# Loading and multiplying the last chunk of an output projection in two parts (8 and 4 rows per partition)

## The chip, the cores and the metric

The kernel runs on one core of one Trainium2 chip. The metric is the device time of one execution in microseconds (us), the median of several. Three runs of the kernel before gave 296.84 us (296.07 to 297.12).

The traced run of the kernel before, from which all lines of "before" come, is 297.04 us, with a span of 295.2 us. The three jobs of experiments ran on three different chips (2, 12 and 1 in the record), so kernels are compared within a job.

## The reference

It is one decode step: attention over the last 2048 positions of a cache for 32 heads of width 192 and a batch of 2, then a gated feed-forward layer.

```python
x = A_x                                                   # [2, 1, 640]
h = x + attention(layernorm(x), k_cache, v_cache, wq) @ wo      # wo: [6144, 640]
h2 = h + (gelu(n @ w_gate) * (n @ w_up)) @ w_down         # n = layernorm(h), F = 1536
```

## The kernel before

All weights and cache tiles stream through one SBUF ring on one DMA queue, in the order in which they are used. `wo` is cut into four chunks `J` of 8 heads, each loaded by one DMA: 128 partitions, 12 rows of 640 bf16 per partition (15360 B). The last two chunks come behind the last V tile, and the feed-forward weights follow them.

```python
load_wo(2)
load_wo(3)
load_ffn()           # gate, up (15360 B per partition each), down in 4 parts of 3840 B

def load_wo(J):
    load(("wo", J), 2 * 12 * D, A_wo[1536 * J:1536 * (J + 1), :].rearrange("(p kk) n -> p kk n", kk=12),
         lambda v: v.rearrange("p (kk n) -> p kk n", kk=12))
```

`oproj(J)` adds the chunk's 24 small matmuls into one PSUM tile. The first waits for the whole chunk.

```python
def oproj(J):
    wo, wtoks = where["wo", J]
    def fn(e):
        # ... (J == 0 adds the residual)
        for kk in range(12):
            for h in range(2):
                r = 2 * (kk % 2) + h
                ins = e.matmul(m1[32 * r:32 * r + 2, 192:512], lhsT=ot[:, J % 2, kk, :],
                               rhs=wo[:, kk, 320 * h:320 * (h + 1)], start=..., stop=...,
                               tile_position=(0, 32 * r), skip_group_check=True)
        return ins
    pe(fn, R=wtoks + [("ot", J % 2), "xrow", "identb"], X=["m1"])
    # ...
```

The tail of the program is a serial chain: `o_rows(3)`, `oproj(2)`, `o_columns(3)` (which writes `ot`), `oproj(3)`, the row of h (`hrow`), its transposes (`h_columns`), layernorm (`hnT`), gate matmuls, residual matmuls, up matmuls, down matmuls, the copy `yrow`, and the output.

Of the kernel before, what the change touches and what calls it, by code (L numbers as in the profile page):

```python
# [13 lines left out]
D = 640  # L14
# [136 lines left out]
def bass_sequential_preLN__sliding_block_cached__geglu_ffn__decode_kernel(  # L151
# [12 lines left out]
    with ExitStack() as ctx:  # L164

        def sb(name, shape, dt):
            return ctx.enter_context(nc.sbuf_tensor(name, shape, dt))

        def ps(name, shape, dt):
            return ctx.enter_context(nc.psum_tensor(name, shape, dt))  # L170
# [4 lines left out]
        identb = sb("identb", [128, 128], BF16)  # L175
# [27 lines left out]
        xrow = sb("xrow", [128, D], BF16)  # L203
# [24 lines left out]
        ot = sb("ot", [128, 2, 12, B], BF16)  # L228
# [11 lines left out]
        m1 = ps("m1", [128, 512], F32)  # L240
# [6 lines left out]
        where, live, queue, used = {}, [], [], set()  # L247

        def load(key, nbytes, src, shape):


            if pos[0] + nbytes > RING:
                pos[0] = 0
            off, i = pos[0], pos[1]
            pos[0], pos[1] = off + nbytes, i + 1
            queue.append((key, off, nbytes, src, shape, i))

        def pump():
            while queue:
                key, off, nbytes, src, shape, i = queue[0]  # L260
                old = [q for q in live if q[1] < off + nbytes and off < q[1] + q[2]]
                if any(q[0] not in used for q in old):
                    return
                for q in old:
                    live.remove(q)
                queue.pop(0)
                live.append((key, off, nbytes))
                v = shape(ring[:, off // 2:(off + nbytes) // 2])
                toks = [("ring", x) for x in range(off // GRAN, (off + nbytes + GRAN - 1) // GRAN)]
                where[key] = (v, toks)  # L270
                P.op("sp", lambda e, v=v, src=src: e.dma_start(v, src), W=toks + [("sem", i % NSEM)],  # L271
                     dma=f"d{i % NSEM}")

        def done(*keys):
            used.update(keys)
            pump()
# [14 lines left out]
                load(("wq", i), 2 * (c1 - c0) * HQ * DH, wq[:, c0:c1, :], lambda v: v.rearrange("p (c n) -> p c n", n=HQ * DH))  # L291

        def load_wo(J):
            load(("wo", J), 2 * 12 * D, A_wo[1536 * J:1536 * (J + 1), :].rearrange("(p kk) n -> p kk n", kk=12),
                 lambda v: v.rearrange("p (kk n) -> p kk n", kk=12))

        def load_ffn():
            for key, w in (("wg", B_w_gate), ("wu", B_w_up)):
# [8 lines left out]
        def dve(fn, R=(), W=(), X=()):  # L307
            return P.op("dve", fn, R, W, X)
# [4 lines left out]
        def pe(fn, R=(), W=(), X=()):  # L313
            return P.op("pe", fn, R, W, X)
# [10 lines left out]
        def tt(out, a, b, op):  # L325
            return lambda e: e.tensor_tensor(out=out, in0=a, in1=b, op=op)  # L326
# [5 lines left out]
        for g in range(NG):  # L332
            if g > 0 and g + 1 < NG:
                load_k(g + 1)
            load_v(g)
            if g % 4 == 3 and g < NG - 5:
                load_wo(g // 4)
        load_wo(2)
        load_wo(3)
        load_ffn()  # L340
        pump()
# [43 lines left out]
        def _x_T(e):  # L385
# [11 lines left out]
            R=["pi"] + [("bits", k) for k in range(11)], W=["pti"])  # L397
# [211 lines left out]
            dve(lambda e: e.tensor_copy(ot[:, J % 2, :, :].rearrange("p k b -> p (k b)"), m2[:, 0:24]), W=[("ot", J % 2)], X=["m2"])  # L609

        def oproj(J):
            wo, wtoks = where["wo", J]

            def fn(e):
                if J == 0:
                    for h in range(2):
                        e.matmul(m1[32 * h:32 * h + 2, 192:512], lhsT=identb[0:2, 0:2], rhs=xrow[0:2, 320 * h:320 * (h + 1)],
                                 start=True, stop=False, tile_position=(0, 32 * h), skip_group_check=True)
                for kk in range(12):
                    for h in range(2):  # L620
                        r = 2 * (kk % 2) + h
                        ins = e.matmul(m1[32 * r:32 * r + 2, 192:512], lhsT=ot[:, J % 2, kk, :],  # L622
                                       rhs=wo[:, kk, 320 * h:320 * (h + 1)], start=(kk == 1 or J > 0 and kk == 0) and J < 3,
                                       stop=(J != 2 and kk >= 10), tile_position=(0, 32 * r), skip_group_check=True)
                return ins

            pe(fn, R=wtoks + [("ot", J % 2), "xrow", "identb"], X=["m1"])
            done(("wo", J))
            if J == 0:
                dve(lambda e: e.tensor_copy(hrow[0:98, :], m1[0:98, 192:512]), W=["hrow"], X=["m1"])  # L630
            if J == 1:
                dve(tt(hrow[0:98, :], m1[0:98, 192:512], hrow[0:98, :], ALU.add), R=["hrow"], W=["hrow"], X=["m1"])
            if J == 3:
                dve(lambda e: e.tensor_tensor_reduce(out=hrow[0:98, :], in0=m1[0:98, 192:512], in1=hrow[0:98, :], scale=1.0, scalar=0.0,
                                                     op0=ALU.add, op1=ALU.add, accum_out=rs[0:98, :]), R=["hrow"], W=["hrow", "rs"], X=["m1"])
# [19 lines left out]
        for g in range(NG):  # L655
            nxt = g + 1 < NG
            J = g // 4 - 1 if g % 4 == 0 and g > 0 else None
            if nxt:
                transposes(g + 1, 0)
            e_columns(g)  # L660
            if g % 4 == 3:
                z_rows(g // 4)
            if J is not None:
                o_columns(J)
            if nxt:
                transposes(g + 1, 1)
            if J is not None and J < 2:
                oproj(J)
            pv(g)
            if nxt:  # L670
                scores(g + 1)
            if g % 4 == 3 and nxt:
                o_rows(g // 4)
            if nxt:
                softmax(g + 1)
        o_rows(3)
        oproj(2)
        o_columns(3)
        oproj(3)

        h_columns()
# [49 lines left out]
        for i, (f0, f1) in enumerate(WDC):  # L731
            wd, wtoks = where["wd", i]
# [11 lines left out]
        for b, q in ((0, "sp"), (1, "act")):  # L744
            P.op(q, lambda e, b=b: e.dma_start(out[b, 0, :].rearrange("(r n) -> r n", r=4), yrow[b:b + 97:32, :]),
                 R=["y"], W=[("out", b)], dma=f"dout{b}")
# [59 lines left out]
```

## Time and profile before

Three lines of the page of the kernel before: the granted TensorE clock in tenths of full speed and the DMA share in 40 slices, and then the shares of the chain of waits that ended last.

```profile
PEclk9995959997979689977998697979599979599555
DMA  7999999999999999999999999999999999999991
...
DMA 69%; PE 24%; DVE 4%; issue 1%; SPq 1%; ACT 0%; DVEq 0%; ACTq 0%
```

The DMA stream is full from the second slice to the 39th, and the chain that ended last is mostly waiting for it. A change that leaves the bytes alone can only gain where the stream is almost over. The clock is at half speed there, in the last three slices.

The timeline of the kernel before, a few lines of the last 20 us. The columns are start (us from the span's start), duration (us), engine, source line, operation, output and inputs with their shapes, count, and in brackets the idle time before it and what ended that.

```profile
274.81 0.18 DVE L609 CAST ot<-m 128x24 bf16<-128x24 f32 x1 [2.11 <-PE m L605]
...
277.07 1.77 PE L622 MATMUL m<-ring,ot 128*2 128x320 bf16 x24 [2.31 <-DMA ring<-in_A_wo_dram]
...
278.89 0.49 DVE L634 CUSTOM_DVE_ANT_0 hrow<-m,hrow 98x320 f32<-98x320 f32 x1 [3.90 <-PE m L622]
...
287.17 1.83 PE L691 MATMUL ops<-ring,hnT 128*2 128x384 bf16 x20
...
290.76 1.77 PE L737 MATMUL m<-ring,uT 128*2 128x160 bf16 x48 [0.35 <-DVE uT L326]
...
292.58 0.33 DVE L743 CAST yrow<-m 98x160 bf16<-98x160 f32 x1 [1.88 <-PE m L737]
```

`ot` is complete at 274.99. TensorE then has nothing to do until the last `wo` chunk is there, and its 24 matmuls fill 1.77 us ahead of `hrow`. The up matmuls (L691 into `ops`) and the down matmuls (L737) show no DMA as their releaser: their weights were there in time.

When each load is complete does not stand in a line of the profile. I read it from the trace as the last of the 16 semaphore increments of each DMA. The Trainium skill ("DMA: Bandwidth & Descriptors", Why a DMA increments its semaphore by 16 and not by 1) says that only the full 16 mean that all the data is there. For the last `wo` chunk here they come between 273.37 and 276.94 us, and the matmuls start at 277.07.

| landing, us | wo 2 | wo 3 | gate | up | down 1 | down 2 | down 3 | down 4 |
|---|---|---|---|---|---|---|---|---|
| before | 272.34 | 276.94 | 281.53 | 286.15 | 287.35 | 288.50 | 289.65 | 290.81 |

### The profile page before, as it was taken

The numbers are of one execution on the slowest core, as the hardware profiler recorded it, in microseconds if no ns is written. First come the engines' busy times: TensorE is split into PE (matmuls) and PEld (weight loads), VectorE is DVE, ScalarE is ACT, GpSimd is POOL, SyncE is SP. The second block draws the span as 40 slices with busy tenths as digits, with TensorE's granted clock in tenths as the row PEclk, the third lists the DMA queues.
The fourth block names the chain that finished last, engine by engine and source line by source line (L and its number), as shares of the span: only waits on it lengthen the run. The fifth ranks groups of instructions, "written<-read, shape, count | busy, mean of one in ns | idle before, by whom it ended". The sixth has DMA issues, their size and how long they took to land.

```text
span 295.2 us, 4895 instructions
## 1 busy us (share of the span) xinstructions
PE 194.2 (66%) x2141; PEld 152.0 (51%) x2141; DVE 130.2 (44%) x326; ACT 95.6 (32%) x119; POOL 2.7 (1%) x19
## 2 busy tenths in 40 slices
PE   2483467749486398749581686767697667685664
PEld 1461165719284385538450656564666464653332
DVE  5950555615256154435353352525266435254022
ACT  2150134614233063516251323434344334241000
POOL 3000000000000000000000000000000000000000
PEclk9995959997979689977998697979599979599555
DMA  7999999999999999999999999999999999999991
GB/s 277 433 441 437 431 426 422 426 422 433 435 419 442 426 440 426 426 420 426 428 430 426 435 436 425 430 435 426 426 425 436 432 430 425 430 420 424 426 388 73
DMA packets 6521, 122.61 MB, mean 415 GB/s; under 512 B 738, under 2 KB 740, under 8 KB 1252
## 3 DMA queue, kind: packets, MB, share of 16 engines
q1 hardware_dynamic: 6488, 122.29, 97.1%
q8 instruction: 17, 0.28, 0.4%
q14 instruction: 4, 0.03, 0.0%
q10 hardware_dynamic: 12, 0.00, 0.0%
HBM read 122.29 MB, written 0.00 MB: 414 GB/s over the span
## 4 chain that ended last, share of the span: by engine, by line
DMA 69%; PE 24%; DVE 4%; issue 1%; SPq 1%; ACT 0%; DVEq 0%; ACTq 0%
DMA ring<-in_A_k_cache_dram 50%; PE tps L474 17%; DMA ring<-in_A_wo_dram 10%; DMA ring<-in_A_wq_dram 9%; PE m L622 1%; PE ops L572 1%; DVE rq L326 1%; PE m L737 1%; PE sps L691 1%; PE m L605 1%; SPq L271 1%; PE ops L691 1%; PE tps L702 1%; DVE ktr L486 0%; PE m L641 0%
## 5 line engine op out<-in xcount | busy, mean ns | idle before, releaser
L474 PE MATMUL tps<-identf,ring 128*128 128x128 f32 x768 | 115.3, 319 | 50.0 <-DMA ring<-in_A_k_cache_dram 49.3
L474 PEld LDWEIGHTS tps<-identf,ring 128*128 128x128 f32 x768 | 107.2, 168 | 52.7 <-DMA ring<-in_A_k_cache_dram 50.6
L483 ACT ACTIVATE ktr<-tps 128x1024 bf16<-128x1024 bf16 x80 | 79.3, 1023 | 90.5 <-PE tps L474 90.0
L486 DVE COPY ktr<-tps 128x1024 bf16<-128x1024 bf16 x112 | 74.1, 688 | 77.5 <-PE tps L474 76.9
L547 ACT ACTIVATE eexp<-sm,nm 128x512 bf16<-128x512 f32 x16 | 11.5, 721 | 65.2 <-DVE nm L545 65.2
L572 PE MATMUL ops<-ring,ering 128*32 128x384 bf16 x512 | 23.7, 327 | 3.8 <-DMA ring<-in_A_v_cache_dram 3.7
L536 DVE CUSTOM_DVE_ANT_1 sm<-sps,mska 128x512 f32<-128x512 f32 x16 | 11.1, 691 | 34.2 <-PE sps L530 34.2
L530 PE MATMUL sps<-ktr,rq 128*16 128x512 bf16 x384 | 24.8, 390 | 0.3 <-DVE rq L326 0.3
L572 PEld LDWEIGHTS ops<-ring,ering 128*32 128x32 bf16 x512 | 12.4, 96 | 12.1 <-DMA ring<-in_A_v_cache_dram 5.7
L530 PEld LDWEIGHTS sps<-ktr,rq 128*16 128x16 bf16 x384 | 9.4, 88 | 10.7 <-issue 1.0
L543 PE MATMUL m<-mrhs,pm 128*128 128x16 bf16 x16 | 2.9, 183 | 18.1 <-DVE mrhs L322 18.1
L543 PEld LDWEIGHTS m<-mrhs,pm 128*128 128x128 bf16 x16 | 1.5, 96 | 25.8 <-DVE mrhs L322 25.8
L496 PE MATMUL tps<-ring,xnT 128*32 128x384 bf16 x80 | 5.1, 406 | 6.8 <-DMA ring<-in_A_wq_dram 6.8
L326 DVE TENSOR_TENSOR rq<-ops,mask 128x96 bf16<-128x96 f32 x16 | 2.7, 249 | 12.8 <-PE ops L514 12.8
L622 PE MATMUL m<-ring,ot 128*2 128x320 bf16 x96 | 5.3, 371 | 3.9 <-DMA ring<-in_A_wo_dram 3.9
L326 DVE TENSOR_TENSOR ering<-m,mask 128x256 bf16<-128x256 f32 x16 | 6.7, 419 | 2.5 <-PE m L556 2.4
L496 PEld LDWEIGHTS tps<-ring,xnT 128*32 128x32 bf16 x80 | 2.2, 114 | 9.5 <-DMA ring<-in_A_wq_dram 7.9
L378 ACT ACTIVATE lt<-m,eps_t 128x2 f32<-128x2 f32 x2 | 0.5, 262 | 20.2 <-PE m L376 20.2
L556 PE MATMUL m<-sel,eexp 128*128 128x64 bf16 x64 | 4.8, 202 | 1.2 <-ACT eexp L547 1.2
L556 PEld LDWEIGHTS m<-sel,eexp 128*128 128x128 bf16 x64 | 4.4, 106 | 1.6 <-DVE nm L545 1.3
L326 DVE TENSOR_TENSOR orow<-m,wm 128x1536 bf16<-128x1536 f32 x3 | 5.3, 1750 | 0.0
L622 PEld LDWEIGHTS m<-ring,ot 128*2 128x2 bf16 x96 | 2.3, 95 | 5.7 <-issue 2.5
(112 smaller groups left out, 80.7 us busy)
## 6 DMA issues: line engine op xcount, KB each, us to landing
ring<-in_A_k_cache_dram SPq DMA_DIRECT2D x16, 3072.0 KB, 27.5
ring<-in_A_v_cache_dram SPq DMA_DIRECT2D x16, 3072.0 KB, 29.8
ring<-in_A_wo_dram SPq DMA_DIRECT2D x4, 1920.0 KB, 30.9
ring<-in_A_wq_dram SPq DMA_DIRECT2D x2, 3072.0 KB, 21.0
ring<-in_B_w_gate_dram SPq DMA_DIRECT2D x1, 1920.0 KB, 33.9
ring<-in_B_w_up_dram SPq DMA_DIRECT2D x1, 1920.0 KB, 24.5
ring<-in_B_w_down_dram SPq DMA_DIRECT2D x4, 480.0 KB, 26.4
ring<-in_A_wq_dram SPq DMA_DIRECT2D x1, 1536.0 KB, 27.9
```

The costliest lines, as they stand in the source:

```text
L326: return lambda e: e.tensor_tensor(out=out, in0=a, in1=b, op=op)
L474: ins = e.transpose(tps[bi][:, 128 * u:128 * (u + 1)], kv[:, off:off + 128], identf[:, :])
L483: act(lambda e, dst=dst, bv=bv: e.activation(out=dst, in_=bv, func=ACT.Copy), W=[("kt", slot, n)], X=[("t", bi)])
L486: dve(lambda e, dst=dst, bv=bv: e.tensor_copy(dst, bv), W=[("kt", slot, n)], X=[("t", bi)])
L496: ins = e.matmul(tps[0][32 * r:32 * (r + 1), 0:384], lhsT=xnT[:, c, 32 * J:32 * (J + 1)], rhs=wq[:, c - c0, 1536 * J + 384 * r:1536 * J + ...
L530: ins = e.matmul(sps[32 * ch:32 * ch + 16, :], lhsT=rq[:, g, k, :], rhs=ktr[:, g % 2, k // 2, 1024 * ch + k % 2:1024 * (ch + 1):2], start= ...
L536: dve(lambda e: e.tensor_tensor_reduce(out=sm[:, :].rearrange("p (u x) -> p u x", u=4), in0=sps[:, :].rearrange("p (u x) -> p u x", u=4), ...
L547: act(lambda e: e.activation(out=eexp[:, :], in_=sm[:, :], func=ACT.Exp, bias=nm[:, 0:1], scale=1.0, accum_out=zr[:, g // 4 % 2, g % 4:g % ...
L556: ins = e.matmul(o, lhsT=eexp[:, 128 * u:128 * (u + 1)], rhs=sel64[:, :], start=True, stop=True)
L572: ins = e.matmul(ops_[32 * r:32 * (r + 1), 0:384], lhsT=ering[:, g % 4, t, :], rhs=vv[:, 384 * t:384 * (t + 1)], start=(g % 4 == 0 and t < 4),
L622: ins = e.matmul(m1[32 * r:32 * r + 2, 192:512], lhsT=ot[:, J % 2, kk, :], rhs=wo[:, kk, 320 * h:320 * (h + 1)], start=(kk == 1 or J > 0 a ...
L691: ins = e.matmul(bank[32 * r:32 * r + 2, 0:384], lhsT=hnT[:, c, :], rhs=wv[:, c, 384 * r:384 * (r + 1)], start=(c == 0), stop=(c == NC5 - ...
```

## The change

The intent is to multiply 8 of the 12 rows while the other 4 are still coming. The last chunk becomes two DMAs into adjacent parts of the ring, and `oproj` two groups of matmuls, each waiting for its own part.

```diff
         def load_wo(J):
-            load(("wo", J), 2 * 12 * D, A_wo[1536 * J:1536 * (J + 1), :].rearrange("(p kk) n -> p kk n", kk=12),
-                 lambda v: v.rearrange("p (kk n) -> p kk n", kk=12))
+            src = A_wo[1536 * J:1536 * (J + 1), :].rearrange("(p kk) n -> p kk n", kk=12)
+            for i, (k0, k1) in enumerate(wo_parts(J)):
+                load(("wo", J, i), 2 * (k1 - k0) * D, src[:, k0:k1, :], lambda v: v.rearrange("p (kk n) -> p kk n", n=D))
+
+        def wo_parts(J):
+            return ((0, 12),) if J < 3 else ((0, 8), (8, 12))
 ...
         def oproj(J):
-            wo, wtoks = where["wo", J]
+            for i, (k0, k1) in enumerate(wo_parts(J)):
+                wo, wtoks = where["wo", J, i]
 ...
-                for kk in range(12):
+                    for kk in range(k0, k1):
 ...
-                                       rhs=wo[:, kk, 320 * h:320 * (h + 1)], ...
+                                           rhs=wo[:, kk - k0, 320 * h:320 * (h + 1)], ...
 ...
-            pe(fn, R=wtoks + [("ot", J % 2), "xrow", "identb"], X=["m1"])
-            done(("wo", J))
+                pe(fn, R=wtoks + [("ot", J % 2), "xrow", "identb"], X=["m1"])
+                done(("wo", J, i))
```

More of the change, by code (lines that the diff above doesn't have):

```diff
@@ L611, in oproj, with fn @@
         def oproj(J):
-            wo, wtoks = where["wo", J]
-            def fn(e):
-                if J == 0:
-                    for h in range(2):
-                        e.matmul(m1[32 * h:32 * h + 2, 192:512], lhsT=identb[0:2, 0:2], rhs=xrow[0:2, 320 * h:320 * (h + 1)],
-                                 start=True, stop=False, tile_position=(0, 32 * h), skip_group_check=True)
-                for kk in range(12):
-                    for h in range(2):
-                        r = 2 * (kk % 2) + h
-                        ins = e.matmul(m1[32 * r:32 * r + 2, 192:512], lhsT=ot[:, J % 2, kk, :],
-                                       rhs=wo[:, kk, 320 * h:320 * (h + 1)], start=(kk == 1 or J > 0 and kk == 0) and J < 3,
-                                       stop=(J != 2 and kk >= 10), tile_position=(0, 32 * r), skip_group_check=True)
-                return ins
-            pe(fn, R=wtoks + [("ot", J % 2), "xrow", "identb"], X=["m1"])
-            done(("wo", J))
+            for i, (k0, k1) in enumerate(wo_parts(J)):
+                wo, wtoks = where["wo", J, i]
+                def fn(e, k0=k0, k1=k1, wo=wo):
+                    if J == 0:
+                        for h in range(2):
+                            e.matmul(m1[32 * h:32 * h + 2, 192:512], lhsT=identb[0:2, 0:2], rhs=xrow[0:2, 320 * h:320 * (h + 1)],
+                                     start=True, stop=False, tile_position=(0, 32 * h), skip_group_check=True)
+                    for kk in range(k0, k1):
+                        for h in range(2):
+                            r = 2 * (kk % 2) + h
+                            ins = e.matmul(m1[32 * r:32 * r + 2, 192:512], lhsT=ot[:, J % 2, kk, :],
+                                           rhs=wo[:, kk - k0, 320 * h:320 * (h + 1)], start=(kk == 1 or J > 0 and kk == 0) and J < 3,
+                                           stop=(J != 2 and kk >= 10), tile_position=(0, 32 * r), skip_group_check=True)
+                    return ins
+                pe(fn, R=wtoks + [("ot", J % 2), "xrow", "identb"], X=["m1"])
+                done(("wo", J, i))
             if J == 0:
```

## The prediction

> **What bounds the kernel.** The DMA stream. The slices of the page show DMA at 9 tenths from the second to the 39th (415 GB/s mean), and the chain of waits is 69% DMA. The Trainium skill ("DMA: Bandwidth & Descriptors", Specifications) puts the fabric ceiling at 435 GB/s; the trace's 420 to 440 GB/s in full slices agrees. The bytes stay, so only the drain after about 272 us can gain.
>
> **The drain, from the chain and the timeline.** The last wo chunk (heads 24 to 31, 15360 B per partition) lands at 276.94 us by its last semaphore increment, 4.60 us after the chunk before it (272.34). `ot`, the stationary side, is written at 274.99. So TensorE waits 2 us for the load alone. Then 24 matmuls (L622) run 277.07 to 278.84 (1.77 us, 74 ns each, granted clock 0.50), and the rest is a serial chain: hrow, layernorm, gate, up, down, output.
>
> **What the change does.** One DMA of 128 x 15360 B becomes 128 x 10240 B and 128 x 5120 B, and the 24 matmuls become 16 behind the first part and 8 behind the second. Instruction order and ring addresses stay; one DMA issue (about 0.4 us on SP, well ahead) and one PE wait are added.
>
> - Packets: 15360 B takes 0.576 us, 3840 B 0.149 us. Interpolated, 10240 B takes 0.386 and 5120 B 0.196, sum 0.582; times 8 packets per DMA engine that is 0.05 us of extra stream time. These are estimates.
> - Part 1 lands near 272.34 + 8 x 0.386 = 275.4, part 2 near 277.0.
> - 16 matmuls at 74 ns: 275.55 to 276.75, hidden under the wait for part 2. 8 matmuls remain: 277.13 to about 277.75 instead of 278.84. hrow starts 1.1 us earlier.
>
> **How much survives.** The FFN weights still arrive at the stream's pace: gate lands 281.53, up 286.15, the down parts 287.35, 288.50, 289.65, 290.81. Before, all were early: gate needed at 283.56, up at 287.17, the last down part at about 292.1. Shifted by 1.1, gate is needed at 282.4 (fine), up at 286.05 against 286.2 plus the 0.13 us from landing to first matmul, so the up matmuls now wait for their DMA and some 0.25 us is given back; the last down part is needed at about 291.2 against 291.0, just fine. Net: about 0.9 us, 0.3% of the span.
>
> **Predicted time:** 295.9 us, range 295.0 to 296.9 (the three runs before spread over 1.05 us). Chances: faster by over 2% 0.01, within 2% 0.98, slower by over 2% 0.01.
>
> **What would show it.** Right: in the timeline the wo matmuls appear as two groups, 16 starting near 275.5 and 8 near 277.1; hrow starts near 277.8; the up-projection's matmuls are released by the up weights' DMA; the last landing moves by under 0.15 us; output is written about 0.9 us earlier. Wrong: part 1 landing at or after 276.5 (the 16 DMA engines finish one chunk as much as 3.6 us apart, so the slowest decides).
>
> **What would make it wrong.** The granted clock in the last 20 us: 0.50 from 272.6 on in this trace. The Trainium skill ("TensorE: Matmul & The Clock Gate", Part 1) says that the window which sets it is free-running; at full clock there, the 24 matmuls cost less and the gain shrinks. A slower DMA engine by chance of instruction fetches (16 KB packets, about 1 us) can move the stream's end by as much as the whole gain.

## The result, and the profile after

| | before | after |
|---|---|---|
| median, us (6 runs each) | 296.85 | 296.08 |
| range, us | 296.07 to 297.18 | 295.85 to 296.27 |

The ratio is 0.9979 (95% interval 0.9963 to 0.9994). This one is the ratio of the two means. Those of E1 to E8 below lie within 0.0005 of the ratio of the means, except that of E5 (see there). The interval excludes 1.

The same three lines of the page of the kernel after:

```profile
PEclk9996579996979589989779697979689979795555
DMA  7999999999999999999999999999999999999992
...
DMA 69%; PE 24%; DVE 4%; SPq 1%; issue 1%; ACT 0%; DVEq 0%; ACTq 0%
```

Nothing has changed in the large: the stream is as full and the chain has the same shares. The timeline of the kernel after, the lines that answer to those of before, with the weight loads (PEld) that show the two groups:

```profile
275.52 0.18 DVE L613 CAST ot<-m 128x24 bf16<-128x24 f32 x1 [0.97 <-PE m L609]
275.75 0.63 PEld L627 LDWEIGHTS m<-ring,ot 128*2 128x2 bf16 x16 [0.36 <-DVE ot L613]
275.75 2.01 PE L627 MATMUL m<-ring,ot 128*2 128x320 bf16 x24 [0.28 <-DVE ot L613]
...
277.06 0.10 PEld L627 LDWEIGHTS m<-ring,ot 128*2 128x2 bf16 x8 [0.69 <-DMA ring<-in_A_wo_dram]
...
277.82 0.49 DVE L639 CUSTOM_DVE_ANT_0 hrow<-m,hrow 98x320 f32<-98x320 f32 x1 [2.12 <-PE m L627]
...
286.27 0.10 PEld L696 LDWEIGHTS ops<-ring,hnT 128*2 128x2 bf16 x8 [0.55 <-DMA ring<-in_B_w_up_dram]
...
286.27 1.77 PE L696 MATMUL ops<-ring,hnT 128*2 128x384 bf16 x20
...
289.81 1.77 PE L742 MATMUL m<-ring,uT 128*2 128x160 bf16 x48 [0.34 <-DVE uT L330]
...
291.63 0.33 DVE L748 CAST yrow<-m 98x160 bf16<-98x160 f32 x1 [1.88 <-PE m L742]
```

The timeline merges both groups of matmuls into one line of 24 (2.01 us with the gap inside), but the weight loads stand apart: 16 released by `ot`, and 8 released by the DMA at 277.06. `hrow` starts at 277.82 instead of 278.89, which is 1.07 us earlier. Further down, the up weights' DMA is now a releaser, which it was not before. `yrow` starts 0.95 us earlier, so 0.12 us of the 1.07 was given back on the way. The clock did not help here: the clock records of the two traces show half speed from 272.63 us (before) and from 266.28 us (after) to the end.

| landing, us | wo 2 | wo 3 part 1 | part 2 | gate | up | down 1 | down 2 | down 3 | down 4 |
|---|---|---|---|---|---|---|---|---|---|
| after | 272.36 | 275.45 | 277.02 | 281.60 | 286.23 | 287.43 | 288.59 | 289.75 | 290.91 |

The landings after the split are 0.07 to 0.10 us later than before.

### The profile page after: what moved, and what is told of

Same layout as the page of the kernel before. It is cut to its first block, busy times and chain, and to the rows that moved or that the text cites. A ratio compares the mean times of both kernels' runs of the same rounds, so it can differ in the third digit from the quotient of the medians.

```text
span 294.3 us, 4896 instructions
## 1 busy us (share of the span) xinstructions
PE 198.8 (68%) x2141; PEld 152.4 (52%) x2141; DVE 130.4 (44%) x326; ACT 95.6 (32%) x119; POOL 2.7 (1%) x19
## 4 chain that ended last, share of the span: by engine, by line
DMA 69%; PE 24%; DVE 4%; SPq 1%; issue 1%; ACT 0%; DVEq 0%; ACTq 0%
DMA ring<-in_A_k_cache_dram 50%; PE tps L478 17%; DMA ring<-in_A_wo_dram 10%; DMA ring<-in_A_wq_dram 10%; PE ops L576 1%; DVE rq L330 1%; PE m L627 1%; SPq L271 1%; PE sps L696 1%; PE m L742 1%; PE m L609 1%; PE ops L696 1%; PE tps L707 1%; PE tps L500 1%; PE m L646 0%
## 5 line engine op out<-in xcount | busy, mean ns | idle before, releaser
L576 PE MATMUL ops<-ring,ering 128*32 128x384 bf16 x512 | 25.0, 339 | 3.6 <-DMA ring<-in_A_v_cache_dram 3.4
L534 PE MATMUL sps<-ktr,rq 128*16 128x512 bf16 x384 | 26.0, 404 | 0.4 <-DVE rq L330 0.4
L500 PE MATMUL tps<-ring,xnT 128*32 128x384 bf16 x80 | 5.7, 444 | 7.6 <-DMA ring<-in_A_wq_dram 7.6
L586 DVE COPY osb<-ops 128x192 f32<-128x192 f32 x8 | 2.5, 354 | 5.8 <-PE ops L576 5.8
```

The source lines that it names most:

```text
L500: ins = e.matmul(tps[0][32 * r:32 * (r + 1), 0:384], lhsT=xnT[:, c, 32 * J:32 * (J + 1)], rhs=wq[:, c - c0, 1536 * J + 384 * r:1536 * J + ...
L534: ins = e.matmul(sps[32 * ch:32 * ch + 16, :], lhsT=rq[:, g, k, :], rhs=ktr[:, g % 2, k // 2, 1024 * ch + k % 2:1024 * (ch + 1):2], start= ...
L576: ins = e.matmul(ops_[32 * r:32 * (r + 1), 0:384], lhsT=ering[:, g % 4, t, :], rhs=vv[:, 384 * t:384 * (t + 1)], start=(g % 4 == 0 and t < 4),
```

## The experiments

The theory is this: the gain is the matmul time that is no longer behind the landing of the last `wo` bytes. It shrinks further down because the feed-forward weights arrive when they arrive. The first rival is that the finer DMA itself, or a shifted program layout, made the difference. The second rival is that the granted clock did: the kernel before has two groups of times, an early and a late one (some expectations below call them fast and slow). For the two traces above the second rival is already out, since the kernel after has less full clock in the tail than the kernel before. For the medians it is not.

The runs of the first four experiments shared 11 runs of the kernel before (median 297.00 us), and the next four shared 9 (297.05 us).

### E1: split the load, not the matmuls

```diff
-                pe(fn, R=wtoks + [("ot", J % 2), "xrow", "identb"], X=["m1"])
+                every = [t for j in range(len(wo_parts(J))) for t in where["wo", J, j][1]]
+                pe(fn, R=every + [("ot", J % 2), "xrow", "identb"], X=["m1"])
```

> The load in two parts as in the change, but all 24 matmuls wait for both parts. Overlap theory: no gain, ratio to the kernel before 1.000 (within 0.0015), the 24 matmuls start near 277.1 us in one block and the last weights land at most 0.15 us later than before. Rival (the finer DMA itself, or the shifted layout, makes the gain): ratio about 0.998, like the change.

The median was 297.07 us and the ratio 1.0004 (0.9992 to 1.0016). The timeline of E1 has one block of 24 matmuls again, waiting for the DMA:

```profile
276.96 1.77 PE L627 MATMUL m<-ring,ot 128*2 128x320 bf16 x24 [2.48 <-DMA ring<-in_A_wo_dram]
...
278.79 0.49 DVE L640 CUSTOM_DVE_ANT_0 hrow<-m,hrow 98x320 f32<-98x320 f32 x1 [4.09 <-PE m L627]
```

The first rival falls: two DMAs without the overlap gain nothing. The times say so without any choice of groups: the five runs of E1 (296.92 to 297.27 us) and the five of E4 below (295.98 to 296.37), which has the overlap and ran in the same job, do not meet. The two DMAs cost little too. From the landing of `wo` 2 to the last landing the stream took 18.47 us before, and 18.55 (after) and 18.56 (E1) with one more DMA, so the extra DMA costs about 0.08 us of stream.

### E2: parts of 4 and 8 rows instead of 8 and 4

```diff
-            return ((0, 12),) if J < 3 else ((0, 8), (8, 12))
+            return ((0, 12),) if J < 3 else ((0, 4), (4, 12))
```

> Parts of 4 and 8 rows instead of 8 and 4. Overlap theory: 16 matmuls (1.18 us at 74 ns) remain behind the second landing instead of 8 (0.59 us), so the row of h starts about 0.55 us later than in the change (near 278.4 us) and half of the gain is left: ratio about 0.9988 if the tail has clock 0.5. Rival (any split gives it): ratio 0.998.

The median was 296.57 us and the ratio 0.9980 (0.9967 to 0.9993). The ratio is the rival's 0.998 and not the expected 0.9988, but its interval holds both and it cannot choose. The timeline of E2 does choose:

```profile
275.17 0.70 PE L627 MATMUL m<-ring,ot 128*2 128x320 bf16 x8 [0.28 <-DVE ot L613]
...
277.12 1.23 PE L627 MATMUL m<-ring,ot 128*2 128x320 bf16 x16 [1.24 <-DMA ring<-in_A_wo_dram]
...
278.40 0.49 DVE L639 CUSTOM_DVE_ANT_0 hrow<-m,hrow 98x320 f32<-98x320 f32 x1 [3.29 <-PE m L627]
```

Sixteen matmuls stay behind the second landing and `hrow` starts at 278.40, just where the overlap theory put it. Of the five runs, three took 296.57 to 296.58 and two about 296.0. The three are 0.50 us under the mean of the 8 late runs of the kernel before in the same job (297.08), which is half of what the change gains against late runs (0.94, below). The two early ones moved the ratio; that they are early for the same reason as those of the kernel before was not traced.

### E3: the kernel before against itself

> The kernel before against itself, for the noise and for a second trace. Ratio 1.000 within 0.001. The six runs of before fall in two groups (four at 296.84 to 297.18, two at 296.07 and 296.10). Clock theory: the fast group has full clock for some of the last 20 us; runs in the two groups should then differ in their mean clock, and a trace of a fast one shows clock 1.0 where the last 24 wo matmuls run, with these taking about 0.95 us instead of 1.77. Rival: the stream ends earlier in the fast group.

The median was 296.87 us and the ratio 0.9991 (0.9979 to 1.0004), so an identical kernel may show 0.1% (the plain means of the runs listed give 0.9995). Two of its six runs and three of the 11 beside it were early (spans of 294.5 to 294.7 us, against 295.0 to 295.6). The mean clock over the whole run does not separate them cleanly: early runs had 0.838 to 0.856 and late ones 0.816 to 0.843, and late runs elsewhere had up to 0.852. The traced run was a late one (297.16 us), and yet it had full clock until 277.37:

```profile
277.21 1.66 PE L622 MATMUL m<-ring,ot 128*2 128x320 bf16 x24 [2.34 <-DMA ring<-in_A_wo_dram]
```

Its last `wo` chunk landed at 277.08, later than in any other trace of this kernel, so only 0.16 us of the matmuls ran at full clock. The groups were left for E9 to E12.

### E4: the change, with the up weights in two parts as well

```diff
+WUC = ((0, 3), (3, 5))
 ...
-            load("wu", ...)                     # one load of 5 chunks
+            for i, (c0, c1) in enumerate(WUC):
+                load(("wu", i), 2 * (c1 - c0) * F, w_up[:, c0:c1, :], ...)
 ...         # ffn_in: one group of matmuls per part, each waiting for its own load
```

> The change, plus the up-projection's weights loaded and multiplied in two parts (3 and 2 of 5 chunks). If the wait for the up weights gives back part of the gain, the up matmuls start about 0.15 us earlier than in the change, right behind the residual matmuls, and the output is written 0.1 to 0.15 us earlier; the last down part (landing 290.9) then limits. Ratio to before about 0.9975. Rival (the give-back is no more than trace noise): no shift, output 14.16 us after the row of h starts, as in the change.

The diff above is shortened. The median was 296.05 us and the ratio 0.9972 (0.9960 to 0.9984). The timeline of E4:

```profile
277.66 0.49 DVE L641 CUSTOM_DVE_ANT_0 hrow<-m,hrow 98x320 f32<-98x320 f32 x1 [1.99 <-PE m L629]
...
285.94 1.82 PE L699 MATMUL ops<-ring,hnT 128*2 128x384 bf16 x20
...
289.53 1.92 PE L745 MATMUL m<-ring,uT 128*2 128x160 bf16 x48 [0.34 <-DVE uT L332]
...
291.50 0.33 DVE L751 CAST yrow<-m 98x160 bf16<-98x160 f32 x1 [2.03 <-PE m L745]
```

The up matmuls start 8.28 us after `hrow`, the same as in the kernel before, where the change has 8.45. So the wait for the up weights was real and cost 0.17 us there. But the saving went straight into the next wait: the 48 down matmuls took 1.92 us instead of 1.77, because the last down part landed at 290.84, and `yrow` came 13.84 us after `hrow` where the change has 13.81. The expected shift of the up matmuls came; the expected earlier output did not come from it.

### E5 and E6: keep TensorE busy in the tail, in the kernel before and in the changed one

```diff
+        def warm(n):        # n matmuls into a PSUM bank that the tail doesn't use
+            def fn(e):
+                for k in range(n):
+                    ins = e.matmul(tps[2][:, :], lhsT=identb[:, :], rhs=ktr[:, 0, k % 3, 0:512], start=True, stop=True)
+                return ins
+            pe(fn, R=["identb"] + [("kt", 0, c) for c in range(12)], X=[("t", 2)])
 ...
         o_rows(3)
+        warm(4)
         oproj(2)
         o_columns(3)
+        warm(8)             # 3 in the changed kernel
         oproj(3)
+        warm(2)
 ...                         # and 3, 4, 3, 3 and 1 in other gaps of the tail
```

> The kernel before, with dummy matmuls (128x128 by 128x512, into an unused PSUM bank) in the gaps of TensorE from the last softmax on, to hold the granted clock at 1.0 in the tail; outputs unchanged. Clock theory: the 24 last wo matmuls take about 0.95 us, the row of h starts near 278.1, the chain catches up with the weight stream and ends at its floor (last down part 290.8, then about 0.75 us to the end of the last row copy, so near 291.6): like the fast group of the kernel before, ratio about 0.996 to 0.997. Rival (the tail is bound by its serial chain at any clock): ratio 1.000.

> The changed kernel with the same dummies (3 instead of 8 ahead of the first part). Floor theory: at full clock the change is worth nothing, since both kernels end behind the last weights: same time as the warm kernel before within 0.3 us, although the row of h starts about 0.5 us earlier. Rival (the change saves the same at any clock): 0.9 us less than the warm kernel before.

E5 took 295.93 us (295.76 to 297.22), ratio 0.9961 (0.9947 to 0.9974). That ratio fits its four quicker runs alone; the mean of all five over that of the kernel before is 0.9970. E6 took 295.97 us (295.74 to 296.08), ratio 0.9961 (0.9948 to 0.9973). So with the dummies the change is worth nothing, as the floor theory said, but this agreement is not clean evidence. The trace of E5 fell on its one slower run, of 297.22 us, where the clock dropped to 0.5 at 279.55 and the dummies themselves then delayed the chain. The trace of E6 is the clear one. Its down matmuls in the timeline of E6:

```profile
286.35 0.98 PE L714 MATMUL ops<-ring,hnT 128*2 128x384 bf16 x20 [0.68 <-DMA ring<-in_B_w_up_dram]
...
289.86 0.38 PE L761 MATMUL m<-ring,uT 128*2 128x160 bf16 x12 [0.33 <-DMA ring<-in_B_w_down_dram]
...
291.08 0.38 PE L761 MATMUL m<-ring,uT 128*2 128x160 bf16 x12 [0.85 <-DMA ring<-in_B_w_down_dram]
...
291.52 0.33 DVE L767 CAST yrow<-m 98x160 bf16<-98x160 f32 x1 [2.63 <-PE m L761]
```

With full clock in this stretch the chain runs into the stream three times: at the up weights and at the last two down parts. TensorE idles 0.85 us for the last one, and the end is the landing (291.04) plus the last 12 matmuls and the copy. A faster chain has almost nothing left to win: `yrow` starts only 0.11 us earlier than in the change.

### E7 and E8: finer parts everywhere, without and with the dummies

```diff
-            return ((0, 12),) if J < 3 else ((0, 8), (8, 12))
+            return ((0, 12),) if J < 3 else ((0, 8), (8, 11), (11, 12))
-WDC = ((0, 3), (3, 6), (6, 9), (9, 12))
+WDC = ((0, 3), (3, 6), (6, 9), (9, 11), (11, 12))      # up in two parts as in E4
```

> The change carried on: wo in parts of 8, 3 and 1 rows, up weights in 3 and 2 chunks, last down part in 2 and 1 rows. If both the chain and the last weights bind, the row of h starts near 277.4, the up matmuls start by 285.8, the last part leaves 4 matmuls behind it, and the last row copy ends near 291.6 instead of 291.95: ratio 0.996 to 0.997, some 0.3 us under the change. Rival (more DMAs cost more than they free): no better than the change, 0.998 or more.

> The finer parts and the dummies together. Floor theory: the chain always waits for the last weights, of which 4 matmuls are left: the last row copy ends about 0.15 us earlier than in the warm kernel before, near 291.4. Rival (the chain binds): earlier by 0.4 us or more than the finer kernel without dummies.

E7 took 296.03 us, ratio 0.9966 (0.9953 to 0.9978). E8 took 296.06 us, ratio 0.9967 (0.9954 to 0.9979). In the traces E7's `hrow` starts at 277.50, 0.32 us before the change's, and its last row copy ends at 291.87, 0.09 us before the change's. The last landing moved back to 291.14 (291.27 in E8), so most of what the finer parts freed was spent on the added DMAs. All nine runs of the kernel before in this job were late, so the two ratios must not be set against the 0.9979 of the change, for which two of six were early. Against late runs alone, E7 is 1.01 us under them and the change 0.94. The expected gain of 0.3 us over the change is a miss, and the rival is nearer to the truth in time, though not in the printed ratio. E8 misses too: its last row copy ends at 291.99, where 291.4 was expected and E6 has 291.84. No version beats the change by more than the noise: E4 to E8 all have medians between 295.93 and 296.06.

### E9 to E12: looks for the early group

E9 is the kernel of E5 again, E10 to E12 the kernel before again, one run each.

> A second trace of the kernel before with dummies, whose first trace fell on its one slow run of five. If this one is fast (span 294.0 to 294.3): clock theory expects clock 1.0 through most of 272 to 291, and the down matmuls waiting for the last weights; rival (fast runs have an earlier weight stream) expects the last landing about 0.9 us earlier, near 289.9.

> The kernel before once more, to catch a trace of its fast group (span 294.5 to 294.7). If caught: clock theory expects full clock for part of 272 to 291, shorter matmul groups there, and the same last landing (290.8 to 291.0); rival expects an earlier last landing, near 290.1.

> As the run just before: a trace of the fast group of the kernel before, if it is caught. In a slow run (295.0 or more): clock 0.5 for all of the tail.

> As the two runs just before: a trace of the fast group of the kernel before, if it is caught. In a slow run (295.0 or more): clock 0.5 for all of the tail.

E9 took 296.07 us, E10 297.15, E11 296.33 and E12 296.76; the one run of the kernel before beside them took 296.74 (span 294.8 us). E11 is the early group, caught. The 24 last `wo` matmuls in the timelines of E10, E11 and E12, in this order (E3's line is above):

```profile
277.06 1.77 PE L622 MATMUL m<-ring,ot 128*2 128x320 bf16 x24 [2.11 <-DMA ring<-in_A_wo_dram]
```

```profile
276.95 1.17 PE L622 MATMUL m<-ring,ot 128*2 128x320 bf16 x24 [2.33 <-DMA ring<-in_A_wo_dram]
```

```profile
277.05 1.50 PE L622 MATMUL m<-ring,ot 128*2 128x320 bf16 x24 [2.36 <-DMA ring<-in_A_wo_dram]
```

The half microsecond from 277.00 in the table of windows of the same three runs (busy time of PE, PEld, DVE, ACT and POOL with counts, then granted clock, DMA share and GB/s):

```profile
277.00:277.50 0.50, 0.44 (x8) 0.27 (x12) 0.00 (x0) 0.00 (x0) 0.00 (x0) 0.50 1.08 461
```

```profile
277.00:277.50 0.50, 0.50 (x18) 0.34 (x21) 0.00 (x0) 0.00 (x0) 0.00 (x0) 1.00 0.93 399
```

```profile
277.00:277.50 0.50, 0.45 (x12) 0.32 (x16) 0.00 (x0) 0.00 (x0) 0.00 (x0) 0.88 0.94 399
```

The granted clock there is 0.50, 1.00 and 0.88. The clock records of the trace show where full speed ended: 268.94 in E10, 277.62 in E11 and 277.38 in E12. In E11 0.67 us of the matmuls ran at full clock and they took 1.17 us; in E12 it was 0.33 us and they took 1.50; in E3 0.16 us and 1.66; in E10 none and they took 1.77. The spans follow: 294.5 us for E11, 295.0 for E12 and 295.3 for E3 and E10. The last weights landed at 290.71, 290.79 and 290.83 in E11, E12 and E10, so the stream of the early run was at most 0.12 us earlier, and the rival (some 0.9 us earlier) falls as the main cause. It has a small part: `hrow` starts 0.71 us earlier in E11 than in E10, 0.60 us by the shorter matmuls and 0.11 us by the earlier landing. So in the five traces of the kernel before the time follows how far one clock stretch reaches into these matmuls, and the groups are two ends of a scale: E12 and the run of 296.74 lie between, and against the expectation two runs with spans of 295.0 us and more (E3 and E12) have some full clock in the tail. The untraced runs are put down to the same cause by analogy only; in the second job none of nine runs was early, and why was not tested. E9 (the dummies) had full clock until 279.08 and again from 289.32, and half clock in between. Its chain lost time to the dummies there and made it up in the down matmuls, and the copy ended at 291.92 us, near E6's 291.84 by another way, although `hrow` starts at 277.98 in E9 and at 277.62 in E6. The timeline of E9 shows no wait for the last weights, which the clock theory had expected:

```profile
290.54 1.00 PE L756 MATMUL m<-ring,uT 128*2 128x160 bf16 x48 [0.35 <-DVE uT L326]
```

That is why the agreement of E5 and E6 is weak evidence.

## Why the prediction was right

- **What bounds it, and what can gain.** Right. The landing before the split did not move (272.34 and 272.36), and the whole gain arises in the last 20 us. The ceiling of 435 GB/s that the prediction cites is met only roughly: the full slices of the trace read 419 to 442 GB/s.
- **Landing of the parts.** Predicted 275.4 and 277.0, measured 275.45 and 277.02. The packets took 0.388 and 0.198 us (median), where 0.386 and 0.196 had been interpolated.
- **The two groups.** Predicted 275.55 and 277.13 with `hrow` near 277.8; measured 275.75, 277.06 and 277.82. The first start was right by 0.2 us but for another reason: in this trace `ot` was ready at 275.70 instead of 274.99, and so the group waited for `ot` and not for the DMA. The clock had dropped at 266.28 rather than 272.63, and E4, where it dropped at 266.73, has a late `ot` too (275.68). That it cost nothing was luck: the 16 matmuls end at 276.99 in the trace (ends of matmuls are modelled there), 0.03 us before part 2 lands.
- **What is given back.** The step was right: the up weights' DMA became the releaser. Its size was set at 0.25 us and came to 0.17 us at the up matmuls and 0.12 us at the end. The term that was too large is the time from landing to first matmul: 0.13 us was assumed, and 0.04 us was measured (286.23 to 286.27). E4 showed that this wait was real, and also that removing it only exposes the next one.
- **The last down part.** "Just fine" was right by a hair. In the change the last 12 of the 48 down matmuls start near 291.14 (three quarters through L742, worked out), and their weights land at 290.91. E4, E6, E7 and E8 all end on that landing.
- **The extra DMA.** Predicted 0.05 us of stream, measured 0.08. The packets explain it: eight times the 0.010 us by which 0.388 and 0.198 exceed 0.576.
- **The total.** Predicted 0.9 us net, and 0.95 us in the traces. The medians show 0.77 and the means 0.63 us, because two of the six runs of the kernel before were early. Against its four late runs (mean 297.00 us) the change (mean 296.06 us) gains 0.94 us, and against its two early ones (296.08 us) 0.02 us. These groups were formed after the fact, by time. And the predicted range of 295.0 to 296.9 us holds the median of the kernel before too, so it is the traces, and not the time, that confirm the mechanism.
- **What would make it wrong.** The caution on the clock was the important one: E11 shows the kernel before at full clock for 0.67 us of the matmuls, with `hrow` at 278.17 instead of 278.89. The Trainium skill ("TensorE: Matmul & The Clock Gate", Part 1) gives a free-running window of 3413 ns; the clock records here agree, with stretches of 3.41, 6.83, 10.24 and 13.65 us and longer multiples, at places that differ from run to run (full speed ends at 272.63, 268.94 and 277.62 us in three traces of the same kernel). The caution on a DMA engine delayed by instruction fetches did not come up, and no run here shows such a delay: in the traces of the kernel before read here the last landing lay between 290.71 and 290.96.

A side effect that the prediction did not name: the six runs of the change spread over 0.42 us and show no two groups, where those of the kernel before spread over 1.11 us. With 8 matmuls behind the landing instead of 24, less work depends on the clock at that moment, and the stream's end stands just below. That this is the whole cause of the smaller spread was not tested by itself, and six runs are few: nine runs of the kernel before in one job spread over only 0.47 us.

## What to carry to other kernels

When a load is the last thing that a chain of small operations waits for, split it so that only a small share of the consuming work is left behind its last byte, and choose the parts from two numbers of the trace: the time per matmul and the time per byte of the stream. Before expecting more, list when every later load lands and when it is needed; here the reserve was 1.3 us at the last load (290.76 plus three quarters of 1.77, less 290.81), so a saving of about 1.1 us nearly used it up and all further splitting gave nothing measurable. When runs of one kernel fall in groups, compare within a group, and look in the trace for what differs just where the critical operation sits: the mean clock over the run hid it.

## What the Trainium skill lacked or had wrong

- "DMA: Bandwidth & Descriptors" (Anatomy of one DMA) gives a fixed cost of about 2 us per DMA, mostly completion latency, for the gpsimd path. No page says what cutting one DMA in two costs inside a full queue. Here, with DMAs issued from the sync engine, it was about 0.08 us of stream per added DMA (18.47 us before, 18.55 and 18.56 with one more, 18.64 in E4 with two more), measured from the landing of `wo` 2 to the last landing.
- The same page (Latency and other measured facts) says that engines 7 and 15 are usually slower, with a guess at the cause that is meant for the gpsimd path alone. Here the 16 increments of the last load of the kernel before fall in two clusters: seven engines at 287.24 to 288.30 us and nine at 290.31 to 290.81 us. So about half of the engines end the stream after the others, on average 2.9 us later. Had all of them ended together, the last weights would have been there some 1.5 us earlier (an estimate: the mean of the 16 increments is 289.31 us), which is more than this change saves; nobody tried it. The runs don't show why the engines differ, and I found it on no page.
- "TensorE: Matmul & The Clock Gate" (Part 1) puts the penalty of the ramp to full clock at under 1% of a typical kernel's span and advises against fitting to one count of slow matmuls. The runs here do not measure the whole penalty. But E10 and E11, the same kernel, differ by 0.82 us (0.3%), most of it by the place of one clock stretch, and that is as large as the whole effect of this change: small differences between kernels can't be judged without it.
